# Layer two's differences of x made and parted earlier, and the early steps' curve and weight work reordered, in a retention and two-layer fp32 kernel

## The chip, the cores and the metric

The kernel runs on one core of a Trainium2 chip. The metric is the device time of one execution in microseconds, lower is better. TensorE (PE), VectorE (DVE), ScalarE (ACT) and GpSimd (POOL) each work through a queue of their own in order; SyncE (SP) issues the transfers. What one engine needs from another it waits for at a semaphore.

## The reference

```
for t in range(S):                                    # per batch and head, S = 768, D = 64
    state = gamma * state + outer(k[t], v[t])
    y[t] = scale * q[t] @ state
x = y as (1536, 512)
x = softplus(x @ w_in) @ w_out                        # layer one, 512 -> 2048 -> 512
r = maximum(x @ moe2_w_in, 0)
out = (s * r * r + b) @ moe2_w_out                    # layer two, 512 -> 2048 -> 512
```

All of it is fp32 (the weights come in as float64 bit patterns). There are 2 batches of 8 heads.

## The kernel before, in words

**Parts.** A matmul operand in full fp32 is carried as two fp32r parts, a high one (`xh`, `wh`, `gh`) and a low one (`xl`, `wl`, `gl`). The high part is a copy by ACT (`split`, L112, or a line of its own), the low part is the source less the high part, a subtraction on POOL or DVE (L115 in `split`). A product is then three matmuls: high by high, high by low, low by high.

**Weights.** A weight half is 128 x 512 values that arrive as 64-bit words in a tile `raw`. `split_w` makes an fp32 tile `wm` out of each with four DVE instructions (L287, L291, L296, L302), a square on ACT between them (L294), and then the two parts, `wh` on ACT and `wl` on POOL. It is a generator, run piece by piece: `fill(n)` runs n pieces in the first part of the program, `go(work, n)` in the later parts. Just behind L296 it also issues the load of a later half (`load_next`), on SP. `wm` has two buffers.

**Retention and the first layer-one steps.** The retention is cut into 24 units (12 chunks of 128 rows, two halves of heads each). `unit(n, ...)` issues the matmuls of a unit (L190), the high part of its x on ACT (`x_hi`, L222), its state on DVE and ACT (L245 or L243, L254, L261) and the low part on DVE (`x_lo`, L228); `score_to` issues later units' score matmuls (L174) and their mask on DVE (L178). Eight units run first. Then each of the first eight layer-one steps `s` holds two units: `early(s)` for steps 0 to 2, `mixed(s)` from step 3 on. A step's `h_mm` is 12 matmuls (L354) into the PSUM bank `h`, and the softplus curve of that bank is made by `act_0` (DVE, L361), `act_1` (ACT, L367) and `act_2` (DVE, L371, the bank's last reader); `act_hi` and `act_lo` part the result into `gh` and `gl`. All eight steps use the same bank `h`, so `h_mm` of step s waits for `act_2` of step s - 1. From step 3 on `acc_mm` (L405, 12 matmuls) folds step s - 3 into the sums, with the second-matrix half of the weight (the fifth half that is split).

**Layer two's differences of x.** From its second pair of hidden blocks on (`second(1, p)`) layer two multiplies 2 x 2 blocks by Strassen's scheme in its Winograd form, which needs four differences of blocks of x, made by `sum_x(k)` on DVE (L446 for k = 3, two instructions; L449 for the others, one of 128 x 1024). `parts_x(k)` parts each into `x1h`, `x1l` and so on: the high part on ACT, the low part in two subtractions on POOL, but on DVE for k = 3 in layer two (L490). They are made while `plain(1, 0)`, layer two's first pair, runs. It has six slots; a slot is 12 matmuls into a bank, the curve of that bank (begun by L528, `begin`), 12 or more matmuls of older work, and then the lists `sums[k]` and `parts[k]` of that slot. The two last slots work on the third tile of x, which the end of layer one (`end`, in slot 2) has just parted.

**The first stretch of `second(1, 1)`.** A product is copied out of bank `h` (`kept`, the tile p1), another is added to it (`joined`, on DVE, L521), and the curve of the sum follows on ACT. The next part fills bank `y`, copies it out on ACT into p5 (`kept`, L510), and the part after that fills bank `y` again, which must wait for that copy. In ACT's queue the copy stands behind the whole curve of the sum.

The order on each engine is that of the code (`manual_schedule`), so a list such as `parts` sets what stands in front of what.

Of the kernel before, what the change touches and what calls it, by code (L numbers as in the profile page):

```python
# [48 lines left out]
def tile_retention_mlps(ctx: ExitStack, tc: tile.TileContext, qk, kv, w1, w2, sb, consts, out):  # L49
# [19 lines left out]
    def bank(pool, tag):  # L69
        return pool.tile([P, 512], F32, tag=tag, name=tag)  # L70
# [110 lines left out]
    def att_out(n, y):  # L181
        ci, f = divmod(n, HF)
        c = ci % NC_B
        t, a = kv_t[ci], a_t.pop(n)
        first, last = c == 0, c == NC_B - 1
        done = set()

        def mm(h, to, cols, l, r):

            nc.tensor.matmul(  # L190
                y[to][h * D : (h + 1) * D, cols], l, r, start=h not in done, stop=True, skip_group_check=True
            )
            done.add(h)

        both = [(i, f * HP + i, h) for i in range(HP) for h in range(2)]

        def inner():
            for i, p, h in both:
                e = slice((2 * p + h) * D, (2 * p + h + 1) * D)
                mm(h, 0, slice(i * C, (i + 1) * C), t[:, 1, e], a[:, h, i * C : (i + 1) * C])  # L200

        def update():
            for i, p, h in both:
                e = slice((2 * p + h) * D, (2 * p + h + 1) * D)
                mm(h, 1, slice(i * D, (i + 1) * D), t[:, 0, e], v2_t[ci][:, 2 * p + h])

        if not first:
            for i, p, h in both:
                mm(h, 0, slice(i * C, (i + 1) * C), st[:, p, h * D : (h + 1) * D], q2_t[ci][:, p])
        inner()  # L210
        if not last:
            update()
        y_t[n] = y
# [6 lines left out]
    def x_hi(n):  # L220
        j, ps, ts_ = where(n)
        nc.scalar.activation(  # L222
            xh[j][:, ps, ts_], y_t[n][0].rearrange("p (i t) -> p i t", i=HP), AF.Copy
        )
# [46 lines left out]
        nc.sync.dma_start(out=t.rearrange("p a b -> p (a b)"), in_=(w1, w2)[layer][f, :, i].bitcast(U32))  # L271
        raw_t[w, i] = t

    def split_w(w, i, pause):

        wh = wp.tile([P, DM], F32R, tag=f"wh{i}", name=f"wh{i}")
        wl = wp.tile([P, DM], F32R, tag=f"wl{i}", name=f"wl{i}")
        t = raw_t.pop((w, i))
        lw, hw = t[:, :, 0], t[:, :, 1]

        if bank_2:
            x = bank_2[0].bitcast(U32)
        else:
            x = (un[:, i] if spare() else word()).bitcast(U32)
        m = dp.tile([P, DM], F32, tag="wm", name="wm")

        nc.vector.tensor_scalar(  # L287
            out=x, in0=hw, scalar1=3, scalar2=0x3FFFFFF8, op0=ALU.logical_shift_left, op1=ALU.bitwise_and
        )
        yield  # L290
        nc.vector.scalar_tensor_tensor(  # L291
            out=x, in0=hw, scalar=cu[:, 0:1], in1=x, op0=ALU.bitwise_and, op1=ALU.bitwise_or
        )
        nc.scalar.activation(m, hw.bitcast(F32), AF.Square)  # L294
        yield
        nc.vector.scalar_tensor_tensor(  # L296
            out=x, in0=lw, scalar=cu[:, 1:2], in1=x, op0=ALU.logical_shift_right, op1=ALU.bitwise_or
        )
        load_next()
        yield  # L300

        nc.vector.scalar_tensor_tensor(  # L302
            out=m, in0=m, scalar=TINY_SQ, in1=x.bitcast(F32), op0=ALU.is_ge, op1=ALU.mult
        )
        m_t[w, i] = m
        if pause:
            yield
        split(wh, wl, m, nc.scalar, nc.gpsimd)
        w_t[w, i] = (wh, wl)

# [34 lines left out]
    def h_mm(s):  # L345
        j = steps[s][2]
        wh, wl = w_t[block(s), 0]
        h_t[s] = bank(ps_h, "h") if s < SB or s % 2 == 0 else bank(ps_y, "y")
        ps = h_t[s]

        ops = [(w, r, cc) for cc in range(KC) for w, r in ((wh, xh), (wh, xl))]
        ops += [(wl, xh, cc) for cc in range(KC)]
        for i, (w, r, cc) in enumerate(ops):
            nc.tensor.matmul(  # L354
                ps, w[:, cc * P : (cc + 1) * P], r[j][:, cc, :], start=i == 0, stop=i == len(ops) - 1
            )
# [9 lines left out]
    def act_1(s):  # L366
        nc.scalar.activation(l_t[s], l_t[s], AF.Softplus)  # L367
# [111 lines left out]
    def parts_x(k, la=1):  # L479
        hi, lo = both(k)  # L480
        if k == 3 or k == 4 and not la:
            src = [x3[c] for c in range(2)]
            for c in range(2):
                nc.scalar.activation(hi[:, c], src[c], AF.Copy)
        else:
            nc.scalar.activation(hi, x_t[k], AF.Copy)
            src = [x_t[k][:, c] for c in range(2)]
        eng = nc.vector if la and k == 3 else nc.gpsimd
        for c in range(2):
            eng.tensor_tensor(out=lo[:, c], in0=src[c], in1=hi[:, c].bitcast(F32), op=ALU.subtract)  # L490
        x_t[k] = hi, lo

    def six(ps, w, x, start):
# [146 lines left out]
    def split_next(to):  # L640

        x = nxt[0]
        if x is None or halves.index(x) >= to:
            return iter(())
        nxt[0] = next(splits, None)
        if x[1] > 1:
            sums_of_w.append((sums_w, split_sums)[x[1] - 2](x[0]))
            return sums_of_w[-1]
        return split_w(*x, pause=True)

    def go(work, n):
        for _ in range(n):
# [1 line left out]

    scored = [0]

    def unit(n, y, mid=lambda: None):

        att_out(n, y)
        x_hi(n)  # L660
        mid()
        if n == 1:
            state_out(0)
        if n < N0:
            decay(n - 1)
        state(n)
        if n > 0:
            state_out(n)
        if n >= N0:
            decay(n - 1)  # L670
        x_lo(n)
        ci, f = divmod(n, HF)
        if f == 0 and ci + 1 < NCHUNK:
            scale_q(ci + 1)
            scale_v(ci + 1)
        if f == HF - 1 and ci + NIN < NCHUNK:
            load_qk(ci + NIN)
            if ci == 0:
                load_next()
            load_kv(ci + NIN)  # L680
# [13 lines left out]
    def out_of(y):  # L694
        return y[:, :HC], y[:, HC : HC + HP * D]
# [3 lines left out]
    def fill(n):  # L699

        for _ in range(n):
            if not left[0]:
                if nxt[0] is None or fill.at < slot_free(*nxt[0]):
                    return
                work[0] = split_w(*nxt[0], pause=False)
                nxt[0] = next(splits, None)
                left[0] = 4
            next(work[0], None)
            left[0] -= 1

    with tc.manual_schedule():
# [28 lines left out]
        for n in range(N0):  # L740
            if n >= len(ys):
                ys.append(bank(*((ps_h, "h"), (ps_y, "y"))[n % 2]))
            unit(n, out_of(ys[n]))
            if n == 1:
                load_next()
                load_next()
                nc.sync.dma_start(out=sbt, in_=sb)
                warm(ac[3], "s2")

            score_to((2, 4, 5, 6, 7, 8, 9, 10)[n], lent)  # L750
            fill((0, 0, 0, 1, 1, 1, 1, 4)[n])

        def early(s):

            fill.at = s
            n = N0 + HF * s
            h_mm(s)
            act_0(s)
            unit(n, out_of(bank(ps_y, "y")), lambda: act_1(s))
            score_to(n + 3, lent)  # L760
            act_2(s)
            act_3(s)
            unit(n + 1, out_of(ac[3]))
            act_hi(s)
            score_to(n + 4, lent)
            fill(4)
            act_lo(s, nc.gpsimd)

        def mixed(s):

            old = s - LAG_U
            fill.at = s
            n = N0 + HF * s
            h_mm(s)
            act_0(s)
            unit(n, out_of(bank(ps_y, "y")), lambda: act_1(s))
            score_to(n + 3, own)
            act_2(s)
            act_3(s)
            act_hi(s)  # L780
            fill(2)
            acc_mm(old, FIRST + SECOND)
            unit(n + 1, out_of(bank(ps_y, "y")))
            score_to(n + 4, own)
            act_lo(s, nc.gpsimd)
            if steps[old][3] == FG - 1:
                for cc in range(KC):
                    take_out(old, cc)
            fill(2)

        def all_x0():
            for k in (1, 2, 4, 3):
# [109 lines left out]
        def second(la, p):  # L902
# [6 lines left out]
            s1, s2, s3, s4 = ((sh[:, k], sl[:, k]) for k in range(4))  # L909
            b11, b21 = ((xh[0][:, k : k + 2], xl[0][:, k : k + 2]) for k in (0, 2))  # L910
            b22 = xh[1][:, 2:4], xl[1][:, 2:4]
            t1, t2, t3, n4 = (x_t[k] for k in (1, 2, 3, 4))

            one, other, third = bank(ps_h, "h"), bank(ps_y, "y"), bank_2[1]

# [34 lines left out]
            go_last()  # L950

            part(base + 5)
            six(one, a22, n4, False)
            c21 = begin(la, one, tags=("u2", "p1"))
            end_part()
            go_first()
# [67 lines left out]
            parts_last()  # L1024

        left = [lambda s=s: acc_mm(s, FIRST + SECOND) for s in range(NS - LAG, NS - 1)] + [end]
        plain(1, 0, left, [[sums_1], [], [sums_1], [sums_1], [], []], [(1,), (), (), (2,), (4,), (3,)])
        for p in range(1, PAIRS):
            second(1, p)
        p = PAIRS - 1  # L1030
# [76 lines left out]
```

## Time and profile before

| | |
|---|---|
| time, 3 runs | 577.04, 578.0, 578.62 us, median 578.0 |
| the profiled execution | 578.15 us, of which its span on the engines is 576.4 |
| mean granted TensorE clock | 0.996 |
| busy, share of the span | PE 564.4 us (98%), DVE 412.0 (71%), ACT 338.3 (59%), POOL 337.9 (59%) |

PE is the engine to look at, and its 98% leaves 12 us of the span in which it did nothing. A difference of the time by well under 12 us can come from where these lie, and from stretches in which PE is busy but at a lower clock. The other engines are far from full over the span, so for them it matters only where in the span they are full, and what stands in front of what in their queues.

### The profile page before, as it was taken

The numbers are of one execution on the slowest core, as the hardware profiler recorded it, in microseconds if no ns is written. First come the engines' busy times: TensorE is split into PE (matmuls) and PEld (weight loads), VectorE is DVE, ScalarE is ACT, GpSimd is POOL, SyncE is SP. The second block draws the span as 40 slices with busy tenths as digits, with TensorE's granted clock in tenths as the row PEclk, the third lists the DMA queues.
The fourth block names the chain that finished last, engine by engine and source line by source line (L and its number), as shares of the span: only waits on it lengthen the run. The fifth ranks groups of instructions, "written<-read, shape, count | busy, mean of one in ns | idle before, by whom it ended". The sixth has DMA issues, their size and how long they took to land.

```text
span 576.4 us, 8120 instructions
## 1 busy us (share of the span) xinstructions
PE 564.4 (98%) x2968; PEld 461.7 (80%) x2968; DVE 412.0 (71%) x621; ACT 338.3 (59%) x616; POOL 337.9 (59%) x284
## 2 busy tenths in 40 slices
PE   7999999999999999999999998999999999999997
PEld 6777787888878878888888886888888888888885
DVE  4889788776786968997879687576675766755324
ACT  3656654444565555543437686858586766667560
POOL 3447675666679696843525696656564646557030
PEclk9999999999999999999999998999999999999999
DMA  8986212202131212332121031222212122100005
GB/s 323 415 319 205 75 38 73 74 1 75 38 109 36 74 47 99 99 105 90 38 73 53 25 106 45 65 74 73 74 61 86 37 78 69 38 0 1 0 7 213
DMA packets 14871, 50.59 MB, mean 88 GB/s; under 512 B 1776, under 2 KB 1776, under 8 KB 14832
## 3 DMA queue, kind: packets, MB, share of 16 engines
q1 hardware_dynamic: 14832, 50.08, 25.4%
q8 instruction: 23, 0.38, 0.3%
q14 instruction: 16, 0.13, 0.1%
HBM read 46.93 MB, written 3.15 MB: 87 GB/s over the span
## 4 chain that ended last, share of the span: by engine, by line
PE 77%; POOL 5%; DVE 5%; DMA 5%; ACT 5%; issue 2%; SPq 0%; DVEq 0%; POOLq 0%
PE acc L582 27%; PE acc L405 11%; PE h L496 8%; PE h L354 6%; PE y L504 5%; PE third L504 5%; PE y L496 4%; PE y L354 4%; DMA qk<-qk 3%; PE y L190 2%; DMA raw<-w 2%; PE third L496 2%; POOL c L556 2%; PE h L504 1%; POOL gl L115 1%
## 5 line engine op out<-in xcount | busy, mean ns | idle before, releaser
L592 DVE TENSOR_TENSOR xa<-acc,xa 128x512 f32<-128x512 f32 x132 | 82.4, 683 | 86.2 <-PE acc L582 86.0
L115 POOL TENSOR_TENSOR wl<-wm,wh 128x512 fp32r<-128x512 f32 x64 | 84.1, 1314 | 101.4 <-ACT wh L112 101.4
L115 POOL TENSOR_TENSOR gl<-c,gh 128x512 fp32r<-128x512 f32 x69 | 91.1, 1323 | 89.0 <-ACT gh L112 70.9
L582 PE MATMUL acc<-wh,gh 128*128 128x512 f32 x192 | 75.2, 392 | 0.0
L582 PE MATMUL acc<-wh,gl 128*128 128x512 f32 x192 | 75.0, 390 | 0.0
L112 ACT ACTIVATE gh<-c 128x512 fp32r<-128x512 f32 x69 | 43.6, 632 | 16.3 <-POOL c L556 11.7
L582 PE MATMUL acc<-wl,gh 128*128 128x512 f32 x192 | 52.5, 389 | 0.0
L112 ACT ACTIVATE wh<-wm 128x512 fp32r<-128x512 f32 x64 | 39.8, 621 | 16.0 <-DVE wm L302 16.0
L294 ACT ACTIVATE wm<-raw 128x512 f32<-128x512 f32 x64 | 42.1, 658 | 7.1 <-POOL wl L115 7.0
L582 PEld LDWEIGHTS acc<-wh,gh 128*128 128x128 f32 x192 | 36.3, 189 | 8.4 <-DVE xa L592 0.4
L582 PEld LDWEIGHTS acc<-wh,gl 128*128 128x128 f32 x192 | 36.2, 189 | 7.5
L291 DVE SCALAR_TENSOR_TENSOR word<-raw,cu,word 128x512 uint32<-128x512 uint32 x54 | 40.8, 756 | 1.9
L582 PEld LDWEIGHTS acc<-wl,gh 128*128 128x128 f32 x192 | 36.0, 188 | 7.5
L302 DVE SCALAR_TENSOR_TENSOR wm<-wm,word 128x512 f32<-128x512 f32 x54 | 37.1, 688 | 6.0 <-ACT wm L294 0.9
L296 DVE SCALAR_TENSOR_TENSOR word<-raw,cu,word 128x512 uint32<-128x512 uint32 x54 | 40.5, 750 | 0.8
L554 ACT ACTIVATE c<-c,sbt 128x512 f32<-128x512 f32 x48 | 39.2, 817 | 1.6
L528 ACT ACTIVATE c<-c 128x512 f32<-128x512 f32 x21 | 13.3, 632 | 45.6 <-DVE c L521 45.3
L405 PE MATMUL acc<-gh,wh 128*128 128x512 f32 x96 | 38.3, 399 | 0.0
L582 PE MATMUL acc<-gl,wh 128*128 128x512 f32 x96 | 37.7, 393 | 0.0
L582 PE MATMUL acc<-gh,wh 128*128 128x512 f32 x96 | 37.6, 392 | 0.0
L405 PE MATMUL acc<-gl,wh 128*128 128x512 f32 x96 | 37.5, 390 | 0.0
L287 DVE TENSOR_SCALAR word<-raw 128x512 uint32<-128x512 uint32 x54 | 37.0, 686 | 0.5
(222 smaller groups left out, 1407.2 us busy)
## 6 DMA issues: line engine op xcount, KB each, us to landing
raw<-w SPq DMA_DIRECT2D x64, 512.0 KB, 3.7
qk<-qk SPq DMA_DIRECT2D x12, 512.0 KB, 8.1
kv<-kv SPq DMA_DIRECT2D x12, 512.0 KB, 8.2
out<-xa SPq DMA_DIRECT2D x12, 256.0 KB, 2.1
cst<-consts SPq DMA_DIRECT2D x1, 518.0 KB, 4.3
cst<-consts SPq DMA_DIRECT2D x1, 256.0 KB, 6.5
sbt<-sb SPq DMA_DIRECT2D x1, 1.0 KB, 9.4
```

Of the source, the lines that this page charges most:

```text
L112: nc.scalar.activation(hi, src, AF.Copy)
L115: lo_eng.tensor_tensor(out=lo, in0=src, in1=hi.bitcast(F32), op=ALU.subtract)
L291: nc.vector.scalar_tensor_tensor(out=x, in0=hw, scalar=cu[:, 0:1], in1=x, op0=ALU.bitwise_and, op1=ALU.bitwise_or)
L294: nc.scalar.activation(m, hw.bitcast(F32), AF.Square)
L296: nc.vector.scalar_tensor_tensor(out=x, in0=lw, scalar=cu[:, 1:2], in1=x, op0=ALU.logical_shift_right, op1=ALU.bitwise_or)
L354: nc.tensor.matmul(ps, w[:, cc * P : (cc + 1) * P], r[j][:, cc, :], start=i == 0, stop=i == len(ops) - 1)
L405: nc.tensor.matmul(acc_t[la, g, j][cc], *ops[i], start=f4 == 0 and i == 0, stop=ends(s) and i == 2)
L496: nc.tensor.matmul(ps, w[a][:, k * P : (k + 1) * P], x[b][:, k], start=start and i == 0, stop=i == len(ops) - 1, skip_group_check=True,)
L504: nc.tensor.matmul(ps, w[a][:, k * P : (k + 1) * P], (xh, xl)[b][j][:, k], start=i == 0, stop=i == len(ops) - 1)
L554: nc.scalar.activation(c, c, AF.Identity, scale=sbt[:, 0:1], bias=sbt[:, 1:2])
L582: nc.tensor.matmul(acc_t[la, p, "pair", j][cc], *ops[i], start=half == 0 and i == 0, stop=half == 1 and i == 2)
L592: nc.vector.tensor_tensor(out=dst, in0=ps, in1=dst, op=ALU.add)
```

## The change

Four things are changed. In `plain(1, 0)` the third difference of x is made in slot 0 as before, the second in slot 1 instead of slot 2, and both are parted in slot 1 (`(3, 2)`), where the second was parted in slot 3 and the third in slot 5; the fourth is made in slot 3 as before and parted there instead of in slot 4. The low part of the third difference is a POOL subtraction now, like the others. In `early(s)` the whole curve (`act_1`, `act_2`) is issued ahead of the unit's `x_hi`, with two pieces of weight work between its halves. And a weight half always has five pieces instead of four: the parts are a piece of their own, which `early` issues behind `x_hi`. The numbers of pieces per unit and step are changed to suit, so that at the end of step 2 five halves are split, as before.

```
-        if pause:
-            yield
+        yield
         split(wh, wl, m, nc.scalar, nc.gpsimd)
...
-        eng = nc.vector if la and k == 3 else nc.gpsimd
         for c in range(2):
-            eng.tensor_tensor(out=lo[:, c], in0=src[c], in1=hi[:, c].bitcast(F32), op=ALU.subtract)
+            nc.gpsimd.tensor_tensor(out=lo[:, c], in0=src[c], in1=hi[:, c].bitcast(F32), op=ALU.subtract)
...
-    def unit(n, y, mid=lambda: None):
+    def unit(n, y, before=lambda: None, mid=lambda: None):
 
         att_out(n, y)
+        before()
         x_hi(n)
         mid()
...
-            fill((0, 0, 0, 1, 1, 1, 1, 4)[n])
+            fill((0, 0, 0, 2, 1, 1, 1, 2)[n])
...
         def early(s):
...
-            unit(n, out_of(bank(ps_y, "y")), lambda: act_1(s))
+
+            def curve():
+                act_1(s)
+                fill(2)
+                act_2(s)
+
+            unit(n, out_of(bank(ps_y, "y")), curve, lambda: fill(1))
             score_to(n + 3, lent)
-            act_2(s)
             act_3(s)
+            fill(2 if last else 0)
             unit(n + 1, out_of(ac[3]))
             act_hi(s)
             score_to(n + 4, lent)
-            fill(4)
+            fill(3 if last else 2)
             act_lo(s, nc.gpsimd)
...
-            fill(2)
+            fill(3)
...
-        plain(1, 0, left, [[sums_1], [], [sums_1], [sums_1], [], []], [(1,), (), (), (2,), (4,), (3,)])
+        plain(1, 0, left, [[sums_1], [sums_1], [], [sums_1], [], []], [(1,), (3, 2), (), (4,), (), ()])
```

PE's queue is the same row for row. On DVE, this is what stood in step 0, from the first piece of the second weight half to `act_2`:

```order
L287 TENSOR_SCALAR acc_113<-raw 128x512
L291 SCALAR_TENSOR_TENSOR acc_113<-raw,cu,acc_113 128x512
L296 SCALAR_TENSOR_TENSOR acc_113<-raw,cu,acc_113 128x512
L302 SCALAR_TENSOR_TENSOR wm<-wm,acc_113 128x512
L361 TENSOR_SCALAR t_443<-h 128x512
L245 TENSOR_TENSOR sm<-sg,y 128x128
L228 TENSOR_TENSOR xl_107<-y,xh_104 128x2x128
L178 TENSOR_TENSOR a<-s,cst 128x512
L371 SCALAR_TENSOR_TENSOR t_474<-h,t_443 128x512
```

And this stands there with the change (the lines past L306 of the file are numbered one lower, so that L360 and L370 are the old L361 and L371):

```order
L287 TENSOR_SCALAR acc_113<-raw 128x512
L291 SCALAR_TENSOR_TENSOR acc_113<-raw,cu,acc_113 128x512
L360 TENSOR_SCALAR t_437<-h 128x512
L296 SCALAR_TENSOR_TENSOR acc_113<-raw,cu,acc_113 128x512
L302 SCALAR_TENSOR_TENSOR wm<-wm,acc_113 128x512
L370 SCALAR_TENSOR_TENSOR t_457<-h,t_437 128x512
L245 TENSOR_TENSOR sm<-sg,y 128x128
L228 TENSOR_TENSOR xl_107<-y,xh_104 128x2x128
L178 TENSOR_TENSOR a<-s,cst 128x512
```

The first reader of the bank (L361) went ahead of two weight instructions, and its last reader (L371) ahead of the unit's state, low part and mask; steps 1 and 2 change in the same way. In step 2 the first two instructions of the next weight half moved up from the end of the step to between its two units.

On POOL, in layer two's first pair, this stood from the last sum of weights of the first slots on (`sl` is the low part of those sums):

```order
L321 TENSOR_TENSOR ws<-wm,ws 128x256
L115 TENSOR_TENSOR gl<-c,gh 128x512 x2
L115 TENSOR_TENSOR wl_3211<-wm,wh_3210 128x512
L115 TENSOR_TENSOR sl<-ws,sh 128x512 x2
L490 TENSOR_TENSOR x2l<-xa_110,x2h 128x512 x2
L115 TENSOR_TENSOR gl<-c,gh 128x512
L490 TENSOR_TENSOR x4l<-xa_110,x4h 128x512 x2
L115 TENSOR_TENSOR gl<-c,gh 128x512
L115 TENSOR_TENSOR wl_3308<-wm,wh_3307 128x512
```

With the change it is:

```order
L320 TENSOR_TENSOR ws<-wm,ws 128x256
L488 TENSOR_TENSOR x3l<-p_3117,x3h 128x512
L488 TENSOR_TENSOR x3l<-u_3119,x3h 128x512
L488 TENSOR_TENSOR x2l<-xa_110,x2h 128x512 x2
L115 TENSOR_TENSOR gl<-c,gh 128x512 x2
L115 TENSOR_TENSOR wl_3223<-wm,wh_3222 128x512
L115 TENSOR_TENSOR sl<-ws,sh 128x512 x2
L488 TENSOR_TENSOR x4l<-xa_110,x4h 128x512 x2
L115 TENSOR_TENSOR gl<-c,gh 128x512 x2
L115 TENSOR_TENSOR wl_3319<-wm,wh_3318 128x512
```

Four subtractions stand at the head now, two of them new to POOL. On DVE, the end of the last slot and the start of `second(1, 1)` was

```order
L302 SCALAR_TENSOR_TENSOR wm<-wm,word 128x512
L490 TENSOR_TENSOR x3l<-p_3117,x3h 128x512
L490 TENSOR_TENSOR x3l<-u_3119,x3h 128x512
L521 TENSOR_TENSOR c<-third,p_3369 128x512
L287 TENSOR_SCALAR word<-raw 128x512
```

and is

```order
L302 SCALAR_TENSOR_TENSOR wm<-wm,word 128x512
L519 TENSOR_TENSOR c<-third,p_3369 128x512
L287 TENSOR_SCALAR word<-raw 128x512
```

The two subtractions ahead of `joined` are gone. On ACT the copies for `x3h` and `x2h` went from the last slot and from slot 3 to slot 1, and `x4h` from slot 4 to slot 3. In SP's queue the fifth weight load stands one chunk earlier, ahead of the loads of the seventh chunk (`qk`, `kv`).

## Rows read from the trace of the kernel before

**Rows 1.** Windows: length, then busy PE, PEld, DVE, ACT, POOL, clock, DMA, GB/s.

```profile
23.92:49.63 25.71, 23.96 (x240) 19.13 (x240) 23.34 (x42) 14.82 (x38) 12.16 (x11) 1.00 0.84 317
49.63:343.13 293.50, 293.37 (x1464) 238.45 (x1463) 236.65 (x341) 160.65 (x295) 193.01 (x155) 1.00 0.21 68
...
352.80:356.50 3.70, 3.70 (x11) 2.88 (x10) 1.41 (x3) 0.63 (x1) 3.62 (x5) 0.54 0.00 0
```

**Rows 2.** PE in order of time, early steps: start, duration, [idle before <-releaser].

```profile
23.92 0.50 PE L354 MATMUL h<-xh,wh 128*128 128x512 f32 x1 [0.55 <-ACT wh L112]
...
31.21 0.50 PE L354 MATMUL h<-xh,wh 128*128 128x512 f32 x1 [0.47 <-DVE t L371]
...
38.10 0.50 PE L354 MATMUL h<-xh,wh 128*128 128x512 f32 x1 [0.53 <-DVE t L371]
...
44.79 0.50 PE L354 MATMUL h<-xh,wh 128*128 128x512 f32 x1 [0.75 <-DVE t L371]
...
49.63 0.50 PE L405 MATMUL acc<-gh,wh 128*128 128x512 f32 x1
```

**Rows 3.** DVE in order of time, steps 0 and 1.

```profile
29.34 0.29 DVE L245 TENSOR_TENSOR sm<-sg,y 128x128 f32<-128x128 f32 x1 [0.37 <-ACT xh L222]
...
31.26 0.29 DVE L245 TENSOR_TENSOR sm<-sg,acc 128x128 f32<-128x128 f32 x1
31.46 0.42 DVE L228 TENSOR_TENSOR xl<-acc,xh 128x256 fp32r<-128x256 f32 x1
31.80 0.68 DVE L178 TENSOR_TENSOR a<-acc,cst 128x512 f32<-128x512 f32 x1
32.40 0.69 DVE L287 TENSOR_SCALAR acc<-raw 128x512 uint32<-128x512 uint32 x1
33.12 0.75 DVE L291 SCALAR_TENSOR_TENSOR acc<-raw,cu,acc 128x512 uint32<-128x512 uint32 x1
33.91 0.76 DVE L296 SCALAR_TENSOR_TENSOR acc<-raw,cu,acc 128x512 uint32<-128x512 uint32 x1
34.77 0.69 DVE L302 SCALAR_TENSOR_TENSOR wm<-wm,acc 128x512 f32<-128x512 f32 x1
```

**Rows 4.** ACT in order of time, step 3: the fifth weight half's high part.

```profile
48.87 0.63 ACT L112 ACTIVATE wh<-wm 128x512 fp32r<-128x512 f32 x1 [1.56 <-DVE wm L302]
```

**Rows 5.** DMA issues of 19.1 to 19.3 us: KB each, us to landing.

```profile
qk<-qk SPq DMA_DIRECT2D x1, 512.0 KB, 9.0
```

**Rows 6.** PE in order of time, layer two's second pair.

```profile
347.67 1.07 PE L582 MATMUL acc<-wl,gh 128*128 128x512 f32 x4
351.53 0.50 PE L496 MATMUL y<-xh,sh 128*128 128x512 f32 x1 [2.79 <-ACT p L510]
...
358.72 0.39 PE L496 MATMUL h<-x4h,wh 128*128 128x512 f32 x1
```

**Rows 7.** DVE in order of time, layer two's first slots and its second pair.

```profile
322.70 2.63 DVE L425 TENSOR_TENSOR acc<-acc,xa 128x512 f32<-128x512 f32 x4 [4.51 <-PE acc L405]
...
330.67 2.48 DVE L449 TENSOR_TENSOR xa<-xa,xa 128x1024 f32<-128x1024 f32 x2
...
343.23 1.69 DVE L490 TENSOR_TENSOR x3l<-p,x3h 128x512 fp32r<-128x512 f32 x1
...
346.54 0.68 DVE L521 TENSOR_TENSOR c<-third,p 128x512 f32<-128x512 f32 x1
```

**Rows 8.** ACT in order of time, there.

```profile
324.17 2.06 ACT L431 ACTIVATE xh<-acc 128x512 fp32r<-128x512 f32 x4 [4.96 <-DVE acc L425]
...
347.26 0.63 ACT L528 ACTIVATE c<-c 128x512 f32<-128x512 f32 x1 [3.16 <-DVE c L521]
...
348.31 0.65 ACT L294 ACTIVATE wm<-raw 128x512 f32<-128x512 f32 x1
```

**Rows 9.** POOL in layer two's first pair, in order of time.

```profile
324.01 0.74 POOL L321 TENSOR_TENSOR ws<-wm,ws 128x256 f32<-128x256 f32 x1
```

**Rows 10.** Line L115 from 317 to 350 us: ns least/median/most, first and last start.

```profile
L115 POOL TENSOR_TENSOR gl<-c,gh x5: 1283/1300/2104, 319.3 to 344.3; 128x512 fp32r<-128x512 f32 x5
```

More of the change, by code (lines that the diff above doesn't have):

```diff
@@ L272, in load_w, with split_w @@
         raw_t[w, i] = t
-    def split_w(w, i, pause):
+    def split_w(w, i):
         wh = wp.tile([P, DM], F32R, tag=f"wh{i}", name=f"wh{i}")
@@ L648, in split_next @@
             return sums_of_w[-1]
-        return split_w(*x, pause=True)
+        return split_w(*x)
     def go(work, n):
@@ L704, in fill @@
                     return
-                work[0] = split_w(*nxt[0], pause=False)
+                work[0] = split_w(*nxt[0])
                 nxt[0] = next(splits, None)
-                left[0] = 4
+                left[0] = 5
             next(work[0], None)
@@ L756, in early @@
             n = N0 + HF * s
+            last = s == LAG_U - 1
             h_mm(s)
             act_0(s)
-            unit(n, out_of(bank(ps_y, "y")), lambda: act_1(s))
+            def curve():
[3 more added lines that the diff above has]
+            unit(n, out_of(bank(ps_y, "y")), curve, lambda: fill(1))
             score_to(n + 3, lent)
-            act_2(s)
             act_3(s)
+            fill(2 if last else 0)
             unit(n + 1, out_of(ac[3]))
@@ L775, in mixed @@
             act_0(s)
-            unit(n, out_of(bank(ps_y, "y")), lambda: act_1(s))
+            unit(n, out_of(bank(ps_y, "y")), mid=lambda: act_1(s))
             score_to(n + 3, own)
@@ L911, in second @@
             b22 = xh[1][:, 2:4], xl[1][:, 2:4]
-            t1, t2, t3, n4 = (x_t[k] for k in (1, 2, 3, 4))
+            t1, t2, t3 = (x_t[k] for k in (1, 2, 3))
             one, other, third = bank(ps_h, "h"), bank(ps_y, "y"), bank_2[1]
@@ L952, in second @@
             part(base + 5)
-            six(one, a22, n4, False)
+            six(one, a22, x_t[4], False)
             c21 = begin(la, one, tags=("u2", "p1"))
```

## Prediction

> **What bounds the kernel now.** I looked first at the windows, for stretches in which PE is idle or its clock is low. From 49.63 to 343.13 us PE is busy 293.37 of 293.50 us at full clock [rows 1]: nothing is to be had there unless PE is given fewer matmuls, and it isn't. The change touches the two places that are left.
>
> The first is the early steps, 23.92 to 49.63 us. PE is busy 23.96 of 25.71 us, and DVE 23.34 [rows 1]: two engines are nearly full at once. In PE's own order of time each step's first matmul comes late, step 0 by 0.55 us for a weight's high part, steps 1 to 3 by 0.47, 0.53 and 0.75 for the curve's last DVE instruction [rows 2]. That is 2.30 us.
>
> The second is layer two's second pair. The last group of matmuls before it starts at 347.67, four of them in 1.07 us; with the last one's tail of 0.39 (the duration of the matmul at 358.72) that is 0.227 each, so the next was due at 348.58. It starts at 351.53, when ACT has copied p out of its bank [rows 6]. Behind the wait the granted clock is 0.54 over 3.70 us [rows 1], that is about 1.2 GHz, and from 351.53 to 358.72 the 24 matmuls there (6, 6 and 12) take 7.19 us where 24 x 0.227 is 5.45. The place costs 2.95 + 1.74 = 4.69 us.
>
> **The change, early part.** *The first wait.* Step 0 waits for the first half's high part. With five pieces spread over units 3 to 6 its last DVE instruction (L302) is issued a unit earlier, and the high part, still behind unit 6, finds it done; so the 0.55 goes and step 0 starts at 23.37.
>
> *The curve.* What PE itself needs from one step's start to the next, its wait taken off [rows 2], is 31.21 - 23.92 - 0.47 = 6.82, then 6.36 and 5.94, and 4.84 from step 3's start to its fold at 49.63. Unhindered it would stand at 30.19, 36.55, 42.49 and 47.33. Whether DVE keeps up is worked out by its queue, with distances from start to start [rows 3]: state 0.20, low part 0.34, mask 0.60, L287 0.72, L296 0.86; L302, L361 and L371 0.60 like the mask, whose duration they have; L291 0.79 where the next one waits for its result, and about 0.70 where another stands between, as it does now. Step 0's twelve matmuls end near 26.4 (12 x 0.227 and a tail). Then L361, L296, L302 and L371 take 2.66; ACT's softplus, as long as its other 512-wide instructions (0.63 [rows 4]), fits beneath L296 and L302 (1.46). The state of unit 8 starts at 29.06, where it was 29.34. From there to unit 9's state the way goes through ACT and back, 31.26 - 29.34 = 1.92 [rows 3], so 30.98. Then DVE has no pause up to the fifth half's L302: 3 states, 5 low parts, 5 masks, 3 L287, 3 L291, 3 L296, 2 L361, 2 L302, 2 L371 are 0.60 + 1.70 + 3.00 + 2.16 + 2.10 + 2.58 + 3 x 1.20 = 15.74 us. On this way the last reader of the bank ends at 36.28 in step 1 and 42.24 in step 2, just ahead of PE's 36.55 and 42.49: the three waits go.
>
> *The new wait.* The fifth half is the one that the first fold reads. Its L302 starts at 30.98 + 15.74 = 46.72 and ends 0.69 later, its high part takes 0.63 more with two hand-overs of some 0.05, and the fold starts at 48.14; PE would be there at 47.33 and waits 0.8. Before, the copy ended at 48.87 + 0.63 = 49.50 [rows 4] and the fold began at 49.63 without a wait. So the early part gives 49.63 - 48.14 = 1.5 us, and not 2.3: the rest goes to DVE, which was as late as PE. Behind it DVE, ACT and POOL are each about as much earlier as PE, in the old order, so the full stretch to 343 moves along. The bounds are 0 (DVE no earlier than before) and 2.3 (no wait at the fold).
>
> *The load.* The fifth weight load goes ahead of the seventh chunk's two loads. One of those takes 9.0 us from an issue at 19.2 [rows 5], so it landed at 28.2; one more of that size ahead of it costs it 1.65 us at the 317 GB/s of this stretch [rows 1], to 29.9. Its first readers are step 1's scores, behind step 1's start (30.2 now) and its twelve matmuls of 0.227, so not ahead of 32.9. This costs nothing, with 3 us of cover; each microsecond past that would be one of PE's.
>
> **The change, layer two.** *What goes from DVE.* Two x3l subtractions stood ahead of the joined sum, from 343.23 to 346.54 [rows 7]. The sum then takes the place of the first, 3.31 us earlier; it can't come earlier still, since the weight instructions ahead of it in DVE's queue don't move. ACT's curve behind it started at 347.26 [rows 8] and the copy of p ended just ahead of 351.53 [rows 6]; both move by 3.31, to 343.95 and 348.2. PE is due at 348.58, so the wait goes, with 0.35 us to spare, and with it the low clock that followed it: 4.69 us.
>
> *What slot 1 takes on.* The sum for x2 (half of the 2.48 us at 330.67) goes into a pause of 4.51 us on DVE; the three ACT copies, four times 512 wide or some 2.1 us by the 2.06 of four such at 324.17, into one of 4.96 us [rows 7, 8]. Neither costs anything as long as slot 2's end-of-layer work finds its inputs as late as now.
>
> *What POOL takes on.* This is the part that could fail. POOL's last sum of weights ended at 324.75 [rows 9]. From there up to the second `wl` of the new list stand 14 subtractions of 128 x 512 at 1.30 [rows 10], 18.2 us. Two DVE sums now meet POOL at work (one in slot 1, one in slot 3). POOL's longest of five such instructions took 2.10 for 1.30 beside the pair of sums at 330.67 [rows 10, 7], so 0.8 is the price of a meeting; 0 to 1.24 (a whole sum) bound it. With 1.6 that `wl` ends at 344.55. The square on ACT that reuses its buffer (L294) was at 348.31 [rows 8] and now comes at 345.0: 0.45 to spare, and 0.35 again behind it before PE waits. What PE itself reads of these fourteen first is a `gl`, in a group that starts 32 matmuls (7.3 us) ahead of 347.67, at 340.4; the two `gl` behind the head of four end before 335, so it costs PE nothing.
>
> The Trainium skill says in SBUF — State Buffer, section Who interferes with whom, that a DVE instruction with both inputs in SBUF and a GpSimd instruction that reads SBUF lock each other out, the one that issues first holding on for its whole length. By that each meeting costs a whole sum, 1.24 us; the `wl` ends at 345.4, the square comes 0.4 late, and PE waits 0.05 us: 572.0 in place of 571.9, and hardly any reserve. The 2.10 agrees in kind and is the smaller price.
>
> **The sum.** Against the profiled execution's 578.15 us: 578.15 - 1.48 - 4.69 = 571.98. The median of the runs shown is 0.15 below that execution, so 571.8 to 572.0 for the median: 571.9. By the bounds of the early part alone 571.0 to 573.4.
>
> **The rivals.** *The early gain is not had* (573.4). For it: DVE is 91% busy there, and my walk has PE and DVE within 0.3 us of each other at two steps. Against it: the fifth half's last instruction really moves up in the count. 0.13. *The early gain is whole* (571.1): PE at the fold at 47.4, if DVE's pauses are shorter than I count, 0.8 us over 16. 0.10. *POOL is late in layer two* (572.4 to 575): each microsecond that POOL loses beyond 2.4 in all (the 1.6 counted and 0.8 to spare) keeps one of PE's wait there, and, when the wait comes near the present 2.8 us, the low clock with it. For it: the list has no pause, and the page's rule eats the reserve. Against it: 1.6 already counts the worst meeting of the rows twice. 0.15. *Another wait takes the place* (576.5 to 578, no change): ACT's queue still has the copy of p behind the whole curve, so anything else that is late there, a weight's high part above all, brings the same wait back, and with it the low clock. Against it: none of those waited. 0.04. *Slower* (580 or more): POOL's fourteen subtractions each go at 2.10 in place of 1.30, since DVE's weight work now runs beside more of them. That is 11 us late at the second `wl`; 9 us reach the copy of p, against the 2.95 that PE waited there before and the 1.5 of the early part. It decides from some 7 us lost on POOL. Against it: the median of those five is 1.30 with DVE's weight instructions running beside them [rows 10]. 0.03.
>
> The forecast has 0.55: 571.3 to 572.5. The range for 8 in 10 takes in both cases of the early part and most of a late POOL, and a little for the spread of the runs: 570.8 to 573.9. A measurement of this kernel tells some 0.3% (1.7 us) from no change. All cases but the last two are faster by more than that: 0.92; within it 0.05; slower 0.03.
>
> **What would show it.** In the profile after: step 0's first matmul at 23.3 to 23.4; no wait of PE for L371's result over 0.2 us in steps 1 to 3; a wait of about 0.8 for the fifth half's `wh` in front of the first fold, which starts near 48.1. In layer two, about 1.5 us earlier on the clock of the trace: no wait in front of the second filling of bank y, and a granted clock of 1.00 there throughout. On POOL the four subtractions at 1.30 or a little more, and the second `wl` over before ACT's square. The forecast is wrong if PE waits for p again, if a step still waits for L371 or the fold comes later than 49, or if a new wait lies in the stretch that was full.

## The result, and the profile after

The changed kernel takes 572.45 us (median of 4 runs, 572.27 to 573.0) against 578.2 us (4 runs, 577.04 to 578.62). The ratio is 0.9905 [0.9888, 0.9923]: it is faster by 1%, and no run of either kernel lies within the range of the other. The profiled execution took 572.27 us, its span is 570.3.

The page of the changed kernel: the span, the busy time of each engine, and PE and its clock in 40 slices.

```profile
span 570.3 us, 8129 instructions
...
PE 562.6 (99%) x2968; PEld 460.8 (81%) x2968; DVE 409.5 (72%) x619; ACT 339.1 (59%) x616; POOL 340.5 (60%) x286
...
PE   8999999999999999999999999999999999999997
...
PEclk9999999999999999999999999999999999999999
```

No slice of the clock is under 9. DVE is 2.5 us less busy than before and POOL 2.6 more, about the two subtractions that changed hands: they took 1.69 [rows 7] and 1.78 us on DVE, of which 0.88 comes back in longer sums (below), and take 1.30 and 1.31 on POOL.

Windows of the changed kernel, with the columns of [rows 1].

```profile
24.00:50.00 26.00, 25.23 (x247) 20.25 (x246) 24.03 (x45) 16.19 (x40) 13.33 (x12) 1.00 0.90 324
50.00:570.00 520.00, 516.40 (x2445) 422.44 (x2444) 371.52 (x543) 309.87 (x537) 315.69 (x260) 1.00 0.20 64
```

In the early stretch PE is idle for 0.77 us where it was idle for 1.75 behind step 0's first matmul, which itself had waited 0.55 [rows 1, 2]. Behind it the clock is 1.00 throughout, where 3.7 us were at 0.54.

PE of the changed kernel in order of time, the rows that answer to [rows 2] and [rows 6].

```profile
23.42 0.50 PE L353 MATMUL h<-xh,wh 128*128 128x512 f32 x1
...
30.16 0.50 PE L353 MATMUL h<-xh,wh 128*128 128x512 f32 x1
...
36.47 0.50 PE L353 MATMUL h<-xh,wh 128*128 128x512 f32 x1
...
42.42 0.47 PE L353 MATMUL h<-xh,wh 128*128 128x512 f32 x1
...
48.09 0.50 PE L404 MATMUL acc<-gh,wh 128*128 128x512 f32 x1 [0.77 <-ACT wh L112]
...
346.10 1.07 PE L580 MATMUL acc<-wl,gh 128*128 128x512 f32 x4
347.01 0.39 PE L494 MATMUL y<-xh,sh 128*128 128x512 f32 x1
...
566.06 0.39 PE L580 MATMUL acc<-wl,gh 128*128 128x512 f32 x1
```

All four waits in front of the steps are gone, the first fold waits 0.77 for the weight's high part, and the second filling of bank y follows without a pause. The last matmul started at 572.33 before and starts at 566.06 now, 6.27 us earlier. The fold is 1.54 us earlier [rows 2], and the other 4.73 lie in layer two.

DVE of the changed kernel in order of time, from the early steps and from layer two's first slots.

```profile
29.14 0.28 DVE L245 TENSOR_TENSOR sm<-sg,y 128x128 f32<-128x128 f32 x1
...
31.00 0.29 DVE L245 TENSOR_TENSOR sm<-sg,acc 128x128 f32<-128x128 f32 x1 [0.66 <-ACT xh L222]
...
46.69 0.69 DVE L302 SCALAR_TENSOR_TENSOR wm<-wm,acc 128x512 f32<-128x512 f32 x1
...
316.71 2.14 DVE L448 TENSOR_TENSOR xa<-xa,xa 128x1024 f32<-128x1024 f32 x1
321.12 2.63 DVE L424 TENSOR_TENSOR acc<-acc,xa 128x512 f32<-128x512 f32 x4 [2.27 <-PE acc L404]
...
329.09 1.22 DVE L448 TENSOR_TENSOR xa<-xa,xa 128x1024 f32<-128x1024 f32 x1
...
341.67 0.69 DVE L519 TENSOR_TENSOR c<-third,p 128x512 f32<-128x512 f32 x1
```

The fifth half's last instruction starts at 46.69. In slot 1 the second sum (2.14) shortens DVE's pause from 4.51 us [rows 7] to 2.27 (the third's, L445, stood ahead of this pause before, too), and L424, the end of layer one, starts when it did: 321.12 against 322.70, with everything behind the fold 1.56 earlier on this clock. The joined sum stands at 341.67 where it was at 346.54, which is 3.31 us earlier beyond that shift.

ACT of the changed kernel in layer two's second pair, against [rows 8].

```profile
342.39 0.63 ACT L526 ACTIVATE c<-c 128x512 f32<-128x512 f32 x1 [1.71 <-DVE c L519]
...
343.45 0.66 ACT L294 ACTIVATE wm<-raw 128x512 f32<-128x512 f32 x1
...
346.04 0.58 ACT L508 ACTIVATE p<-y 128x512 f32<-128x512 f32 x1
```

The copy of p ends at 346.62, and PE wants it at 347.01: 0.39 us to spare.

POOL of the changed kernel, from slot 1 to the second `wl` of the list.

```profile
314.31 3.45 POOL L488 TENSOR_TENSOR x1l<-xa,x1h 128x512 fp32r<-128x512 f32 x2
317.73 2.27 POOL L115 TENSOR_TENSOR gl<-c,gh 128x512 fp32r<-128x512 f32 x1
...
323.43 0.73 POOL L320 TENSOR_TENSOR ws<-wm,ws 128x256 f32<-128x256 f32 x1
324.12 1.30 POOL L488 TENSOR_TENSOR x3l<-p,x3h 128x512 fp32r<-128x512 f32 x1
...
329.16 3.56 POOL L115 TENSOR_TENSOR gl<-c,gh 128x512 fp32r<-128x512 f32 x2
...
338.94 2.55 POOL L115 TENSOR_TENSOR gl<-c,gh 128x512 fp32r<-128x512 f32 x2
341.45 1.29 POOL L115 TENSOR_TENSOR wl<-wm,wh 128x512 fp32r<-128x512 f32 x1
```

One `gl` takes 2.27 for 1.30 beside DVE's sum at 316.71, and two take 3.56 for 2.55 beside the sum at 329.09. These are the two meetings that the change brings. The `wl` ends at 342.74, the square at 343.45 did not wait for it, and 0.7 us are to spare.

### The profile page after: what moved, and what is told of

Its sections match the earlier page's. It is cut to its first block, busy times and chain, and to the rows that moved or that the text cites. A ratio compares the mean times of both kernels' runs of the same rounds, so it can differ in the third digit from the quotient of the medians.

```text
span 570.3 us, 8129 instructions
## 1 busy us (share of the span) xinstructions
PE 562.6 (99%) x2968; PEld 460.8 (81%) x2968; DVE 409.5 (72%) x619; ACT 339.1 (59%) x616; POOL 340.5 (60%) x286
## 4 chain that ended last, share of the span: by engine, by line
PE 93%; DVE 3%; DMA 2%; SPq 1%; ACT 1%; issue 0%; DVEq 0%
PE acc L580 35%; PE acc L404 12%; PE h L494 10%; PE y L502 7%; PE third L502 7%; PE h L353 6%; PE y L494 5%; PE y L353 4%; PE third L494 2%; PE y L190 2%; DMA qk<-qk 2%; PE h L502 2%; PE s L174 1%; DVE acc L296 0%; DVE a L178 0%; DVE acc L291 0%
## 5 line engine op out<-in xcount | busy, mean ns | idle before, releaser
L115 POOL TENSOR_TENSOR wl<-wm,wh 128x512 fp32r<-128x512 f32 x64 | 83.6, 1306 | 98.5 <-ACT wh L112 98.5
L115 POOL TENSOR_TENSOR gl<-c,gh 128x512 fp32r<-128x512 f32 x69 | 91.7, 1332 | 82.1 <-ACT gh L112 61.8
L302 DVE SCALAR_TENSOR_TENSOR wm<-wm,word 128x512 f32<-128x512 f32 x54 | 37.1, 688 | 6.2 <-ACT wm L294 1.2
```

Source lines behind the costliest of these rows:

```text
L115: lo_eng.tensor_tensor(out=lo, in0=src, in1=hi.bitcast(F32), op=ALU.subtract)
```

## The experiments

A time is a median with its lowest and highest run. The experiments ran in three groups on three chips, each group beside the kernel before, whose medians there were 578.48, 578.43 and 578.29 us. Where a kernel is set against one of another group, a stretch within the two traces is the firmer measure.

**One part alone.** The early part without layer two's lists, and layer two's lists without the early part. For the first, these lines of the changed kernel were put back:

```
+        eng = nc.vector if la and k == 3 else nc.gpsimd
         for c in range(2):
-            nc.gpsimd.tensor_tensor(out=lo[:, c], in0=src[c], in1=hi[:, c].bitcast(F32), op=ALU.subtract)
+            eng.tensor_tensor(out=lo[:, c], in0=src[c], in1=hi[:, c].bitcast(F32), op=ALU.subtract)
...
-        plain(1, 0, left, [[sums_1], [sums_1], [], [sums_1], [], []], [(1,), (3, 2), (), (4,), (), ()])
+        plain(1, 0, left, [[sums_1], [], [sums_1], [sums_1], [], []], [(1,), (), (), (2,), (4,), (3,)])
```

> The early steps' reordering alone, layer two's lists and the third difference's DVE subtractions as before. Theory (two separate gains): the fold starts near 48.1 us after a wait of about 0.8 for the fifth half's high part, layer two keeps its wait of 2.8 us and the low clock behind it, and the time is 1.5 us under before, 576.7. Rival (one gain, in layer two only; the early one is given back later): 578.0 to 578.3.

Measured: 576.89 us (575.25 to 577.26, 10 runs), ratio 0.9973 [0.9958, 0.9988]. PE of this kernel at layer two's second pair, and the window behind it:

```profile
350.25 0.50 PE L495 MATMUL y<-xh,sh 128*128 128x512 f32 x1 [2.78 <-ACT p L509]
...
355.84 0.39 PE L495 MATMUL h<-x4h,wh 128*128 128x512 f32 x1
```

```profile
351.00:355.00 4.00, 4.00 (x19) 3.26 (x19) 2.65 (x5) 1.65 (x4) 3.72 (x6) 1.00 0.02 7
```

The wait for p is whole again. But in this execution the clock behind it stayed at 1.00, where it was 0.54 in the execution of before [rows 1]; that is taken up at the end.

The other way round, the same lines of the diff were put into the kernel before.

> Layer two's part alone on the kernel before. Theory: early waits of 0.47 to 0.75 as before, no wait for the copy of p, granted clock 1.00 there, 4.7 us under before, 573.5. Rival (layer two gains only because PE arrives earlier or later there): 575 or more, with part of the wait left.

Measured: 573.76 us (573.5 to 574.23, 4 runs), ratio 0.9926 [0.9903, 0.9948]. PE waits for L371 and for the first high part in the early steps as in [rows 2], and for nothing in layer two; its fold starts at 49.45. In the medians of this group the two parts give 1.59 and 4.72 us, 6.3 together, and the whole change gave 5.75 beside its own runs of the kernel before. They add up, within what these medians can tell. The traces say it more firmly: from step 0 to the fold it takes 24.68 us with the early part alone and 24.67 in the changed kernel, and from the fold to the last matmul 518.09 with layer two's part alone and 517.97 in the changed kernel.

**Which of layer two's edits it takes.** First only the engine: x3l goes to POOL, at its old place in the last slot of the kernel before.

```
-        eng = nc.vector if la and k == 3 else nc.gpsimd
...
-            eng.tensor_tensor(out=lo[:, c], in0=src[c], in1=hi[:, c].bitcast(F32), op=ALU.subtract)
+            nc.gpsimd.tensor_tensor(out=lo[:, c], in0=src[c], in1=hi[:, c].bitcast(F32), op=ALU.subtract)
```

> The kernel before, with one change: the third difference's two low-part subtractions go from DVE to POOL at their old place in the last slot; the lists stay. Theory (POOL's list must also be early): the joined sum comes about 2.4 us earlier, but POOL now stands at the second wl until about 346.9, ACT's square waits for that, and p is copied near 350.1: PE still waits about 1.6 us of its 2.95; 575.1 if the clock stays up, 576.9 if it falls. Rival (only DVE's two subtractions mattered): no wait, 573.5.

Measured: 575.53 us (575.17 to 575.71, 6 runs), ratio 0.9954 [0.9939, 0.9968]. ACT of this kernel at the square, and PE at the second filling:

```profile
347.24 0.67 ACT L294 ACTIVATE wm<-raw 128x512 f32<-128x512 f32 x1 [0.89 <-POOL wl L115]
```

```profile
350.47 0.50 PE L495 MATMUL y<-xh,sh 128*128 128x512 f32 x1 [1.39 <-ACT p L509]
```

DVE is relieved, and half of the wait stays, because POOL's old list brings the `wl` too late for the square and the square stands ahead of the copy of p. So the engine alone is not enough, and POOL has to be early.

This kernel also shows what made the two subtractions long. In the kernel before they took 1.69 [rows 7] and 1.78 us on DVE, where one of the same form takes 0.68 while POOL stands idle, and POOL's two beside them took 1.74 each. DVE and POOL of the kernel before:

```profile
312.21 0.68 DVE L391 TENSOR_TENSOR gl<-t,gh 128x512 fp32r<-128x512 f32 x1
...
344.84 1.78 DVE L490 TENSOR_TENSOR x3l<-u,x3h 128x512 fp32r<-128x512 f32 x1
```

```profile
344.34 1.74 POOL L115 TENSOR_TENSOR gl<-c,gh 128x512 fp32r<-128x512 f32 x1
346.04 1.74 POOL L115 TENSOR_TENSOR wl<-wm,wh 128x512 fp32r<-128x512 f32 x1
```

With DVE's two gone, the same two on POOL take 1.30 and 1.29:

```profile
344.65 1.30 POOL L115 TENSOR_TENSOR gl<-c,gh 128x512 fp32r<-128x512 f32 x1
345.91 1.29 POOL L115 TENSOR_TENSOR wl<-wm,wh 128x512 fp32r<-128x512 f32 x1
```

So of the 3.31 us that stood ahead of the joined sum, an estimated 2 (3.31 less twice 0.68) were the price of running beside POOL, and the change ends that meeting too.

Then the reverse: the changed kernel, with x3l made early, but on DVE.

```
+        eng = nc.vector if la and k == 3 else nc.gpsimd
...
-            nc.gpsimd.tensor_tensor(out=lo[:, c], in0=src[c], in1=hi[:, c].bitcast(F32), op=ALU.subtract)
+            eng.tensor_tensor(out=lo[:, c], in0=src[c], in1=hi[:, c].bitcast(F32), op=ALU.subtract)
```

> The changed kernel, with the third difference's two subtractions on DVE again, in slot 1. Theory (the place matters, not the engine): they lie in DVE's pause of 2.27 us ahead of the end of layer one, which comes 0 to 1.2 us later and has 1.9 us to spare; no wait of PE, 572.4 like the changed kernel. Rival (DVE can't take them there, since they meet POOL's list): the end of layer one is late and PE waits for the third tile's parts, 573.5 or more.

Measured: 573.25 us (573.05 to 573.47, 4 runs), ratio 0.9916 [0.9894, 0.9938]. The theory missed, and its rival came nearer: the median is 0.8 us over the changed kernel's, and from step 0 to the last matmul it takes 543.79 us against 542.64. DVE of this kernel in slots 1 and 2, and PE's new wait:

```profile
318.78 1.78 DVE L489 TENSOR_TENSOR x3l<-p,x3h 128x512 fp32r<-128x512 f32 x1
320.49 1.77 DVE L489 TENSOR_TENSOR x3l<-u,x3h 128x512 fp32r<-128x512 f32 x1
322.19 2.62 DVE L424 TENSOR_TENSOR acc<-acc,xa 128x512 f32<-128x512 f32 x4
324.76 2.48 DVE L432 TENSOR_TENSOR xl<-acc,xh 128x512 fp32r<-128x512 f32 x4
```

```profile
326.19 0.47 PE L581 MATMUL acc<-wh,gh 128*128 128x512 f32 x1 [1.01 <-ACT c L527]
```

Two subtractions fill the pause of 2.27 us and 1.07 more, so the end of layer one is 1.07 late, and PE waits 1.01. The waiting matmul is the first fold of slot 3. By the program it writes a bank in which layer one's sums lay, which ACT (the copies `xh`) and DVE (the first two instructions of L432) must have read; both are late by the same 1.05. The trace names ACT's next instruction as the releaser; which of the two came last was not told apart. In the changed kernel that fold starts at 325.14, without a wait, and the two instructions of L432 end at 324.95 (323.71 and half of 2.48). So behind DVE's pause there is no reserve at all, and the pause itself is all that slot 1 has.

Last, the third difference early on POOL, but the second where it was:

```
-        plain(1, 0, left, [[sums_1], [sums_1], [], [sums_1], [], []], [(1,), (3, 2), (), (4,), (), ()])
+        plain(1, 0, left, [[sums_1], [], [sums_1], [sums_1], [], []], [(1,), (3,), (), (2,), (4,), ()])
```

> The changed kernel, with only the third difference parted early (slot 1, on POOL); the second is made in slot 2 and parted in slot 3, the fourth parted in slot 4, as before. Theory (POOL's idle stretch of slots 1 to 3 has to take both): the third's 2.6 us go into it, but the second's 2.6 us still stand ahead of the second wl, which ends as late as in the run with the third on POOL in the last slot; ACT's square waits for it and PE waits 1.4 us for the copy of p, at full clock as in the two runs with such a wait; 573.9. Rival (the third alone was late, moving the second is idle work): no wait, 572.4.

Measured: 574.44 us (574.07 to 574.72, 4 runs), ratio 0.9936 [0.9918, 0.9954]. POOL of this kernel behind x3l, and PE:

```profile
328.36 1.29 POOL L115 TENSOR_TENSOR gl<-c,gh 128x512 fp32r<-128x512 f32 x1 [1.72 <-ACT gh L112]
331.59 2.09 POOL L115 TENSOR_TENSOR gl<-c,gh 128x512 fp32r<-128x512 f32 x1 [1.94 <-ACT gh L112]
```

```profile
349.51 0.50 PE L494 MATMUL y<-xh,sh 128*128 128x512 f32 x1 [1.37 <-ACT p L508]
```

POOL stands idle for 1.72 and 1.94 us between its first subtractions, and what it could have done there comes later. The second difference, which seems to have nothing to do with the wait for p, fills these pauses in the changed kernel. The profiled execution (574.72) began its first step 0.95 us later than that of the changed kernel (24.37 against 23.42), which covers what it lies above the expectation; the other three took 574.07 to 574.59.

**How much reserve POOL has.** The changed kernel, with the two subtractions of x2l done twice:

```
                 for x in parts[k]:
                     parts_x(x, la)
+                    if la and x == 2:
+                        for c in range(2):
+                            nc.gpsimd.tensor_tensor(
+                                out=x_t[2][1][:, c], in0=xa[1][:, 2 + c], in1=x_t[2][0][:, c].bitcast(F32), op=ALU.subtract
+                            )
```

> The changed kernel, with the second difference's two POOL subtractions made twice (the same values again), 2.56 us more at the head of POOL's list. Theory (POOL's list, ACT's square, the copy of p, PE): the changed kernel has 0.7 us between the second wl and the square and 0.4 between the copy and PE, so about 1.5 us come out as a wait of PE in front of the second filling of bank y: 574.0, and 575.6 if the clock falls behind it. Rival (POOL's list is hidden there): 572.4, no wait.

Measured: 574.0 us (573.74 to 574.06, 4 runs), ratio 0.9929 [0.9908, 0.995]. ACT at the square and PE, of this kernel:

```profile
345.46 0.67 ACT L294 ACTIVATE wm<-raw 128x512 f32<-128x512 f32 x1 [1.76 <-POOL wl L115]
```

```profile
348.70 0.50 PE L494 MATMUL y<-xh,sh 128*128 128x512 f32 x1 [1.37 <-ACT p L508]
```

The square is 2.01 us later than in the changed kernel (343.45), and the matmul 1.69 later than 347.01, that is 2.01 less the 0.39 to spare, within 0.1. The chain from POOL's list over the square and the copy of p to PE is shown by this, with its reserve.

**What in the early part gives the gain.** The changed kernel, with the curve's second half behind the next scores' mask again, and all of the weight pieces as they are:

```
             def curve():
                 act_1(s)
                 fill(2)
-                act_2(s)
...
             score_to(n + 3, lent)
+            act_2(s)
```

> The changed kernel, with the curve's last DVE instruction behind the unit's state, low part and mask again in steps 0 to 2; weight pieces where the change put them. Theory: PE waits for it about 0.3, 0.3 and 1.1 us in steps 1 to 3, the fold starts near 48.9 (48.09 in the changed kernel, 49.63 before) without a wait for the weight, and the time is 0.8 us over the changed kernel, 573.25. Rival (the weight half's DVE work alone sets the fold): fold at 48.1, 572.4.

Measured: 573.39 us (573.35 to 573.45, 4 runs), ratio 0.992 [0.9902, 0.9938]. PE's waits in the steps of this kernel, and its fold:

```profile
30.38 0.47 PE L353 MATMUL h<-xh,wh 128*128 128x512 f32 x1 [0.26 <-ACT sg L261]
...
37.23 0.47 PE L353 MATMUL h<-xh,wh 128*128 128x512 f32 x1 [0.52 <-DVE t L370]
...
44.28 0.47 PE L353 MATMUL h<-xh,wh 128*128 128x512 f32 x1 [1.13 <-DVE t L370]
...
49.12 0.50 PE L404 MATMUL acc<-gh,wh 128*128 128x512 f32 x1
```

The waits of steps 1 to 3 come back, and the one at the fold goes. (At step 1 the profile names L261, a state instruction of ACT, which ends 0.09 us behind the L370 of step 0.) The median is 0.94 longer than in the first runs of the changed kernel. From step 0, here at 23.31, to the fold it takes 25.81 us, against 24.67 in the changed kernel and 25.71 before. So with the weight pieces at their new place but the curve behind the mask, nothing of the 1.04 us that the change gains in this stretch is left. The other half microsecond of the early part's 1.5 lies ahead of step 0: its wait of 0.55 [rows 2], which the weight pieces of the units before take away, is gone here too. The curve at its new place with the weight pieces at the old one was not run, so whether the curve's place would be enough by itself in the steps stays open.

**What the last wait holds.** The changed kernel, with the rest of the fifth half's work in step 2 moved to between unit n + 1's high part and its state, so ahead of that unit's state, low part and mask:

```
-            unit(n + 1, out_of(ac[3]))
+            unit(n + 1, out_of(ac[3]), mid=lambda: fill(3 if last else 0))
...
-            fill(3 if last else 2)
+            fill(0 if last else 2)
```

> The changed kernel, with the fifth half's last three pieces issued between the second unit's high part and its state in step 2, so that state, low part and mask of unit 13 (1.14 us on DVE) come behind them. Theory (the fold waits for DVE): the weight is there near 47.05 and the fold starts at about 47.5, when the mask has read the bank that the fold writes; 0.5 us under the changed kernel, 571.9. Rival (another wait stands right behind): 572.4, with a new wait of PE between 47 and 52 us.

Measured: 572.05 us (571.83 to 572.73, 4 runs), ratio 0.9899 [0.988, 0.9918]. The changed kernel was then run again beside it.

> The changed kernel once more, beside the next run on one chip: 572.4 us.

> The kernel with the fifth half's last three pieces ahead of unit 13's state once more: its fold started at 47.50 against 48.09 and its last matmul at 565.51 against 566.06, so 0.5 us under the changed kernel in the same call, 571.9. Rival (the difference of 0.4 between the medians of two calls was their spread): no difference in one call.

Measured: 572.39 us (572.13 to 572.57, 5 runs) for the changed kernel, ratio 0.99 [0.9884, 0.9916], and 572.14 us (571.69 to 572.29, 5 runs) for this one, ratio 0.9894 [0.9876, 0.9912]. PE of the second of these:

```profile
23.95 0.50 PE L353 MATMUL h<-xh,wh 128*128 128x512 f32 x1
...
48.18 0.47 PE L404 MATMUL acc<-gh,wh 128*128 128x512 f32 x1 [0.35 <-ACT st L254]
```

From step 0 to the fold it takes 24.23 us here (24.24 in the first run of this kernel, 47.50 - 23.26) and 24.67 in both traces of the changed kernel. These 0.43 us stay up to the last matmul. The medians differ by 0.25 and the runs overlap, so the trace shows the gain and the times hardly do. What PE waits for now is the state of the unit that was put behind the weight: moving one piece ahead makes another late.

## Why the prediction was right, and where it was off

**The early part** came as worked out: step 0 at 23.42 (23.37), the steps at 30.16, 36.47 and 42.42 (30.19, 36.55, 42.49), the states of units 8 and 9 at 29.14 and 31.00 (29.06, 30.98), the fifth half's L302 at 46.69 (46.72), a wait of 0.77 at the fold (0.8). The gain was 1.54 us (1.48): DVE was as late as PE, and the walk along its queue gave the place where the rest would stay. That step 0 itself was met to 0.05 is in part luck, since it starts anywhere between 23.26 and 24.37 in the nine traces with the early part. What they show is that its wait is gone in all nine, where it is 0.45 to 0.55 in the three traces without the early part. That the fifth weight load cost nothing fits with no wait of PE for a DMA between step 0 and the fold.

**Layer two** gave 4.73 (4.69). The joined sum moved by the 3.31 us of the two subtractions ahead of it, and the copy of p had 0.39 to spare (0.35). The size holds for an execution of the kernel before in which the clock fell behind the wait, as the profiled one did; not all of them do (see the last section). Of the two terms, the 1.74 for the low clock is a little too large: with the early part alone, at a clock of 1.00, the same 24 matmuls behind the wait take 5.59 us (350.25 to 355.84) and not 5.45, so 1.60 is the clock's and 0.14 goes with the wait.

**The price of a meeting** on POOL was a mis-sized term: 0.97 and 1.01 us, where 0.8 was taken and 1.24 was the upper end. The first pushed the list's start back (its last sum of weights ends at 324.16, where the old 324.75 less the shift of 1.56 is 323.19), the second lies in the list. Still the `wl` was over at 342.74, a little ahead of the 342.99 that the prediction's 344.55 is on this clock. For from start to start a subtraction in the list takes 1.255 and not 1.30, fourteen times; that is 0.63 less, against 0.38 more for the two meetings. So the reserve ahead of the square was 0.7 and not 0.45.

The Trainium skill says in SBUF — State Buffer, section Who interferes with whom, that a DVE instruction with two inputs in SBUF and a GpSimd instruction that reads SBUF contend, and that the one that issues first keeps the other out until it is done. This trace agrees in kind: DVE's sum of 316.71 took 2.14 in place of 1.22 while POOL's x1l ran until 317.76, and POOL's `gl` of 317.73 took 2.27 in place of 1.30 while that sum ran until 318.85. The whole sum of 1.24 as a price was not reached.

**"Neither costs anything"**, said of slot 1, was right for what was put there, but with no cover behind it that the text named: the kernel with x3l early on DVE shows that DVE's remaining 2.27 us are all there is, and each microsecond past them is one of PE's.

**The sum** said 571.98 for the profiled execution, which took 572.27. The last matmul is 6.27 earlier, more than the 6.17 counted. But the span behind it is 0.17 longer (4.24 us against 4.07), and what lies outside the span 0.22 longer (1.97 against 1.75): 578.15 - 6.27 + 0.17 + 0.22 = 572.27. The 0.17 is there in all kernels that have the early part (4.19 to 4.29) and in none of the three without it (4.05 to 4.07); where it comes from stays open.

**The rivals.** The late POOL came only where it was brought about (1.37 us of PE's wait with two more subtractions, 1.37 with the second difference left late, 1.39 with x3l late on POOL), and there without a lower clock. None of the others appeared.

## What to carry to other kernels

A wait of the bottleneck engine is best followed back through the queue of each engine on the way, for what stands ahead of the late instruction; here it was two subtractions that only had to be somewhere else, and taking them off one engine was worth only half of the wait as long as the other engine's list was late too. When a pause is used up, look for who reads the result of the work behind it: the reserve is the pause plus what that reader can wait, and here that was nothing. Two engines that are both nearly full give back only what the second one can follow, which a walk along its queue told to 0.1 us here. An instruction that takes 1.7 us where its like take 0.7 asks for a look at what the other engine does beside it.

## What the runs showed of the hardware

**The clock behind one wait.** After PE's wait of 2.78 to 2.79 us the granted clock does not always fall. Of the 31 runs of the kernel before that stand beside the experiments, 7 had a mean clock of 1.0 and took 576.58 to 577.02 us, 21 had 0.996 or 0.997 (577.99 to 579.0), and 3 had 0.993 (579.46 to 579.79). With the early part alone it was 3 of 10 at 1.0 (575.25 to 575.79) against 7 at 0.997 (576.73 to 577.26). Where the clock falls is seen in one profiled execution, that of the kernel before: there it is the stretch behind this wait, near the lower of its two levels (0.54, with 1.2 GHz at 0.50; [rows 1]). What else fell in the three with 0.993 no trace shows. So some 1.6 us of the gain in the median, as much as the 1.60 of the 24 matmuls, is a fall of the clock that three executions in four had; against the seven without it (median 576.84) the change is worth 4.4 us. After waits of 1.37 to 1.39 us the mean clock was 0.999 or 1.0 in all 14 runs of three kernels. Without the wait the runs also lie closer: 572.13 to 573.0 in the 9 of the changed kernel.

**The start.** Step 0 starts between 23.26 and 24.37 us in the traces of kernels with the same work ahead of it. Ahead of it PE waits for the input loads, and these waits differ from one execution to the next (1.07 us at 7.80 in the changed kernel; 0.39 at 8.11 and 0.93 at 18.02 in the trace that starts at 24.37). A single time can differ by as much as the starts do, which is more than some of the effects here. But from step 0 to the last matmul the two traces of the changed kernel agree to 0.07 us (542.64 and 542.71).
